# Attention and two MoE layers on one core: products with the weights' high halves first, all low halves on GpSimd, the last logits on TensorE

## The chip, the cores and the metric

The kernel runs on one core of one Trainium2 chip. The metric is the time of one execution on the device in microseconds. Engines go by short names: PE (TensorE, matrix products), DVE (VectorE), ACT (ScalarE), POOL (GpSimd) and SP (SyncE, which issues most DMAs).

## What is computed

Attention over pooled keys and values, then two mixture-of-experts layers (MoE 1 and MoE 2), in float32. 4608 tokens of 512 numbers each go to one of 8 experts; an expert is two matrices, 512 x 1024 and 1024 x 512.

```python
scores = scale * np.matmul(q, k_p.transpose(0, 1, 3, 2))      # k_p, v_p: means over 8 positions
...
logits = x @ w_gate                        # MoE 2: + modality_bias[modality_id]
expert_idx = np.argmax(logits, axis=1)
...
gate_w = probs[np.arange(N), expert_idx]   # probs: softmax of the logits
for e in range(E):
    mask = expert_idx == e
    xe = x[mask]
    h = np.maximum(xe @ w1[e], 0.0)
    ye = h @ w2[e]
    out[mask] = gate_w[mask, None] * ye
```

## The kernel before

**Three products for one.** A float32 matrix is held as a high half (ACT casts it to a shorter form, fp32r) and a low half (the rest, a subtraction on DVE or POOL). x w becomes xh wh + xl wh + xh wl. So each weight block that arrives by DMA in a staging tile is split: `w1h` and `w2h` by ACT (L213, L230), `w1l` and `w2l` by a subtraction (L214, L237). Each has four parts of 128 x 1024. In the tables `W1P` and `W2P` stand the parts made on POOL (0, 1, 2 of `w1l`; 0, 1, 3 of `w2l`); the others are made on DVE.

**Blocks.** The tokens of a MoE lie sorted by expert in DRAM (`XS`). `moe_body` works through blocks of 256 rows; 22 in MoE 1 (numbers 0 to 21) and 19 in MoE 2 for this input. An expert's last block can have 128 rows or fewer (a half block): then only half of the work is done, by another branch. In a block:

- rows of the next block, already in `xq`, are transposed on DVE (`xpose`, L223) to `xt`, and split to `xT` by ACT (L226) and POOL (L227);
- `gemm1`, 96 products of 128 x 256: four `ph` tiles (f2 = 0 to 3) of 24 products each, in three PSUM buffers. After each, ACT makes `hh` (ReLU, high half, L273) and DVE `hl` (low half, L274). Within a `ph` tile the three products of each piece follow each other: w1h xh, w1h xl, w1l xh;
- `gemm1_half`, for a half block: 48 products, and then eight transposes, whose results give `hh` (L256) and `hl` (L259);
- `gemm2(1)` and then `gemm2(0)`, 24 products of 128 x 512 each for rows 128 to 255 and 0 to 127, in the order hh w2h, hh w2l, hl w2h for each of 8 pieces. A half block does only `gemm2(1)`;
- the result, scaled by the gate on ACT (L1067), is scattered by POOL (L153): in MoE 1 to the sorted rows of MoE 2, in MoE 2 to the output.

**Gating of MoE 2** runs inside MoE 1, a block late: 16 logits a block on DVE (`logits2`, L1128, a multiplication by a column of the gate's weights with an accumulator, which reads the `py` result from PSUM), then some eleven small operations on DVE (`gate_a1`, `gate_a2`, `gate_b2`: L110 to L150), with rank products on PE (L135, L138). The tiles between them, and the logits `lgz`, lie in SBUF. In each block the order on DVE is fixed by the order of the code: `LH` = 4 of the 8 logits of one half in one place, the others in a later one. The last block's rows stay in SBUF (`tail`); their logits are made in the first block of MoE 2 by `lg_last`: for rows 0 to 127 by four transposes and four products on PE, for rows 128 to 255 by 8 operations on DVE with both inputs in SBUF.

**Change of weights.** When the next block belongs to another expert, a flag from a table lets the engines take branches that split the new weights: `next_w1`, `next_w2` and, after half blocks (flags `phchg` and `hchg`), some in other places. In MoE 1 this happens ahead of blocks 4, 5, 7, 8, 12, 15, 16 and ahead of MoE 2. Blocks 4, 5, 8, 15 and 16 are half blocks.

**The table.** Which rows and which expert a block has is worked out by some 60 small operations on DVE (`table`, L777 to L880). They stand in block 0 and block 1 of each MoE. `load_chg` and `load_regs` read its results (`nbt`) into registers.

The engines run their own instruction streams in order; where one needs another's result it waits at that instruction, with all that stands behind it.

Of the kernel before, what the change touches and what calls it, by code (L numbers as in the profile page):

```python
# [20 lines left out]
def attn_moe_moe(ctx: ExitStack, tc: tile.TileContext, q, k, v, wg1, w1a, w2a, ids, wg2, bias2, w1b, w2b, out):  # L21
# [86 lines left out]
    def gate_a1(lg, ns, valid, oh=None, go=now, dd=None):  # L108
# [33 lines left out]
    def gate_b2(oh, rk, ns, m, ib, rows, go=now):  # L142
        pa = sp.tile([P, ns, E], F32, name=f"pa{ns}", tag=f"pa{ns}")
# [95 lines left out]
    def gemm1_half(xs, early):  # L239
        for g in range(2):  # L240
            ph = mh.tile([P, 2, BK], F32, name="ph", tag="ph")
            for j in range(2):
# [516 lines left out]
    def table(m):  # L759
# [536 lines left out]
```

## Time and profile before

| | |
|---|---|
| device time, three runs | 1207.57, 1210.95, 1212.03 us (median 1210.95) |
| span of the profiled execution | 1206.5 us |
| PE busy (matmul) | 1101.0 us, 91% |
| DVE busy | 730.3 us, 61% |
| POOL busy | 494.6 us, 41% |
| ACT busy | 375.9 us, 31% |

The profiled execution has one time only, its span. Attention fills the first part of it, MoE 1 runs from there to 760 us, MoE 2 from 765 us to the end. The busy shares are means over all of it; the stretches behind them differ. A group of waits tells how long an engine stood still, at which instruction, and which engine's instruction released it. In a timeline, a number with "x" behind an instruction tells how many stand in the row, and the length is that of the row.

### The profile page before, as it was taken

To read this page: it belongs to the slowest core of one execution; us is meant where nothing else is said; L and a number is where in the kernel's file an instruction comes from. 1 tells how busy PE (TensorE), PEld (TensorE's weight loads), DVE (VectorE), ACT (ScalarE), POOL (GpSimd) and SP (SyncE) were. 2 spreads that over 40 slices of the span, in tenths; PEclk is the share of its full clock that TensorE was granted. 3 is DMA by queue.
4 is the path that set the end of the run, shared out by engine and by line. 5 is a ranking of instruction groups with operands and counts; after the bars stand their busy time and mean duration, and the time that the engine had idled before them with its cause. 6 is when DMAs were issued, how large, how long until landed. Compare 5 with 4: busy or idle time off the path is not lost. (4 is left out here: it accounts for less than half of the span.)

```text
span 1206.5 us, 24663 instructions
## 1 busy us (share of the span) xinstructions
PE 1101.0 (91%) x6985; PEld 971.5 (81%) x6985; DVE 730.3 (61%) x1914; ACT 375.9 (31%) x716; POOL 494.6 (41%) x488
## 2 busy tenths in 40 slices
PE   6979998889986989989978999599999999999997
PEld 5767877768975868978857898588989989989986
DVE  4866776788889887887798868772221223221221
ACT  2433444424253441242351223212212232212211
POOL 5455666654176663162484224512121144121221
PEclk8988999888988989999998999989999999999999
DMA  8999667426357474142171721037212112121121
GB/s 206 251 263 269 179 188 197 169 69 138 93 139 214 111 173 124 50 124 89 43 203 39 184 56 55 22 89 178 54 49 60 37 37 71 37 58 51 37 56 37
DMA packets 148620, 135.63 MB, mean 112 GB/s; under 512 B 62502, under 2 KB 116774, under 8 KB 148272
## 3 DMA queue, kind: packets, MB, share of 16 engines
q1 hardware_dynamic: 138448, 104.68, 35.4%
q0 software_dynamic: 9424, 28.47, 6.7%
q8 instruction: 80, 1.31, 0.5%
q14 instruction: 140, 1.15, 0.3%
q10 hardware_dynamic: 528, 0.02, 0.0%
HBM read 249.30 MB, written 39.31 MB: 239 GB/s over the span
## 5 line engine op out<-in xcount | busy, mean ns | idle before, releaser
L270 PE MATMUL ph<-xT,w1h 128*128 128x256 f32 x2112 | 381.8, 283 | 12.9 <-DVE hl L274 7.0
L270 PEld LDWEIGHTS ph<-xT,w1h 128*128 128x128 f32 x2112 | 329.0, 190 | 18.1 <-DVE hl L274 7.4
L270 PE MATMUL ph<-xT,w1l 128*128 128x256 f32 x1056 | 297.4, 282 | 0.0
L1053 PE MATMUL py<-w2h,hl 128*128 128x512 f32 x608 | 247.0, 406 | 22.4 <-DVE hl L259 20.3
L274 DVE SCALAR_TENSOR_TENSOR hl<-ph,hh 128x512 fp32r<-128x512 f32 x140 | 95.3, 686 | 278.8 <-ACT hh L273 238.8
L1053 PE MATMUL py<-w2l,hh 128*128 128x512 f32 x608 | 244.1, 402 | 5.8 <-POOLq L911 4.6
L1053 PE MATMUL py<-w2h,hh 128*128 128x512 f32 x608 | 245.6, 404 | 0.5 <-ACT hh L256 0.5
L227 POOL TENSOR_TENSOR xT<-xt,xT 128x512 fp32r<-128x512 f32 x78 | 100.2, 1305 | 258.3 <-ACT xT L226 247.8
L270 PEld LDWEIGHTS ph<-xT,w1l 128*128 128x128 f32 x1056 | 200.5, 190 | 0.0
L1128 DVE SCALAR_TENSOR_TENSOR xr<-py,mt,wgt 128x512 f32<-128x512 f32 x284 | 194.4, 745 | 6.6 <-DVEq L911 6.0
L273 ACT ACTIVATE hh<-ph 128x512 fp32r<-128x512 f32 x140 | 83.8, 600 | 291.5 <-PE ph L270 266.7
L1053 PEld LDWEIGHTS py<-w2h,hl 128*128 128x128 f32 x608 | 116.8, 192 | 52.5 <-DVE hl L259 22.4
L153 POOL DMA_INDIRECT XS<-xr,pos x84 | 83.1, 989 | 160.1 <-DVE pos L150 66.3
L1053 PEld LDWEIGHTS py<-w2l,hh 128*128 128x128 f32 x608 | 117.1, 193 | 34.9 <-POOLq L911 5.5
L1053 PEld LDWEIGHTS py<-w2h,hh 128*128 128x128 f32 x608 | 117.1, 193 | 26.0 <-ACT hh L256 0.8
L214 POOL TENSOR_TENSOR w1l<-stage,w1h 128x1024 fp32r<-128x1024 f32 x31 | 74.0, 2404 | 58.8 <-ACT w1h L213 58.1
L1069 POOL DMA_INDIRECT out_dram<-yo,oi x37 | 37.2, 1006 | 136.4 <-POOLq L911 67.4
L321 POOL TENSOR_TENSOR stage<-stage 128x512 f32<-128x512 f32 (+4 forms) x60 | 72.2, 1213 | 24.8 <-DMA stage<-in_v_dram 14.4
L223 DVE STREAM_TRANSPOSE xt<-xq 128x1024 f32<-128x1024 f32 x42 | 52.3, 1244 | 46.9 <-POOLq L911 28.4
L237 POOL TENSOR_TENSOR w2l<-stage,w2h 128x1024 fp32r<-128x1024 f32 x32 | 75.5, 2391 | 6.4 <-ACT w2h L230 6.2
L1067 ACT ACTIVATE yo<-py,mt 128x512 f32<-128x512 f32 x37 | 25.5, 689 | 152.6 <-PE py L1053 147.3
L1067 ACT ACTIVATE xr<-py,mt 128x512 f32<-128x512 f32 x39 | 26.8, 688 | 130.5 <-PE py L1053 125.5
(267 smaller groups left out, 1409.8 us busy)
## 6 DMA issues: line engine op xcount, KB each, us to landing
stage<-in_moe_w_dram SPq DMA_DIRECT2D x196, 512.0 KB
stage<-in_moe_w_dram SPq DMA_DIRECT2D x44, 2048.0 KB
xq<-XS SPq DMA_DIRECT2D x180, 128.0 KB
XS<-zero SPq DMA_DIRECT2D x16, 516.0 KB
qp<-in_q_dram SPq DMA_DIRECT2D x32, 256.0 KB
stage<-in_k_dram SPq DMA_DIRECT2D x7, 1024.0 KB
stage<-in_v_dram SPq DMA_DIRECT2D x7, 1024.0 KB
wgt<-WT SPq DMA_DIRECT2D x1, 2048.0 KB
```

Of the source, the lines that this page charges most:

```text
L153: i = nc.gpsimd.indirect_dma_start(out=XS[m][:], out_offset=bass.IndirectOffsetOnAxis(ap=pos[0 : src.shape[0], s : s + 1], axis=0), in_=sr ...
L214: (eng or nc.vector).tensor_tensor(out=w1l[:, j], in0=wst1[:, :, f], in1=w1h[:, j].bitcast(F32), op=ALU.subtract)
L223: nc.vector.transpose(out=dst[:].rearrange("p c (g i) -> p g c i", i=QP), in_=src[:].rearrange("p g (c j) -> p g c j", c=NC1))
L227: (eng or nc.gpsimd).tensor_tensor(out=dst[:, 1, cs], in0=src[:, cs], in1=dst[:, 0, cs].bitcast(F32), op=ALU.subtract)
L237: (eng or nc.vector).tensor_tensor(out=w2l[c], in0=wst2[:, 2 * c : 2 * c + 2, :], in1=w2h[c][:].bitcast(F32), op=ALU.subtract)
L270: nc.tensor.matmul(ph[:, fc % 2, :], lhsT=lw[:, fc // 2, c, fs], rhs=rx, start=n == 0, stop=n == len(mms) - 1)
L273: nc.scalar.activation(out=hh[f2], in_=ph, func=AF.Relu)
L274: nc.vector.scalar_tensor_tensor(out=hl[f2], in0=ph, scalar=0.0, in1=hh[f2][:].bitcast(F32), op0=ALU.max, op1=ALU.subtract)
L321: (eng or nc.gpsimd).tensor_tensor(out=r[0:pp, sl, 0:w], in0=r[0:pp, sl, 0:w], in1=r[0:pp, sl, w : 2 * w], op=ALU.add)
L1053: nc.tensor.matmul(py, lhsT=lw[fc // 2][:, fc % 2, s * P : (s + 1) * P], rhs=rw[fc // 2][:, fc % 2, :], start=n == 0, stop=n == 3 * NC2 - 1)
L1067: nc.scalar.activation(out=x2[:, s, 0:DM], in_=py, func=AF.Copy, scale=t_[:, s, 0:1])
L1128: V.scalar_tensor_tensor(out=junk[e % 2], in0=py, scalar=sc, in1=wgt[:, e, :], op0=ALU.mult, op1=ALU.mult, accum_out=lgz[:, s, e : e + 1])
```

## The change

1. `gemm1_late` takes the place of `gemm1` in all blocks but the first of MoE 1: all products with `w1h` of f2 = 0, 1, 2 (48), then those with `w1l` of these (24), then high and low of f2 = 3. `gemm1_half` and `gemm2` are written likewise: in `gemm2` 16 products with `w2h`, then 8 with `w2l`.
2. All low halves are made on POOL. `next_w1` makes the four w1 parts in one place, after the block's gemm1 and the split of the next rows; `next_w2` the four w2 parts in one place, after `gemm2(0)`. The places for half blocks, their flags and four operations of the table are gone.
3. The gate's scratch (`lgz`, `lg2`, a copy of `rev`, `m2`, `pa`, `pf`) lies in a PSUM tile `gsc`, so that the operations of the gate have an operand in PSUM.
4. `lg_last` makes the logits of both halves of the last rows on PE.
5. `LH` is 5; the other logits follow after the low products of f2 = 2, or after gemm1 in a half block. In block 0 of MoE 2 gate steps and w2 splits stand at other places.

```diff
+    def gemm1_late(xs, each):
+        phs = {}
+        for low, f2 in ((0, 0), (0, 1), (0, 2), (1, 0), (1, 1), (1, 2), (0, 3), (1, 3)):
+            if not low:
+                phs[f2] = mh.tile([P, 2, BK], F32, name="ph", tag="ph")
+            ph = phs[f2]
+            for h in range(2):
...
+            if low:
+                nc.scalar.activation(out=hh[f2], in_=ph, func=AF.Relu)
+                nc.vector.scalar_tensor_tensor(out=hl[f2], in0=ph, scalar=0.0, in1=hh[f2][:].bitcast(F32), op0=ALU.max, op1=ALU.subtract)
+                each(NC2 + f2)
...
-        def next_w1(*js):
-            if nxt < NB or m == 0:
-                gated(nxt_chg(), lambda: [split_w1(j, nc.gpsimd if j in W1P else None) for j in js])
+        def next_w1():
+            if i > 0 and (nxt < NB or m == 0):
+                gated(nxt_chg(), lambda: [split_w1(j, nc.gpsimd) for j in range(4)])
...
-        if i > 2:
-            gated(phchg, lambda: [split_w2l(c, nc.gpsimd if c in W2P else None) for c in range(4)])
...
+            seq = [(lw, w2h, fc) for fc in range(NC2) for lw in (hh, hl)] + [(hh, w2l, fc) for fc in range(NC2)]
...
-            logits2(1, x[:, 1, 0:DM], 1.0, range(E))
+            for h in range(2):
+                for c in range(NC1):
+                    nc.tensor.transpose(tp[h][:, c * P : (c + 1) * P], x[:, h, c * P : (c + 1) * P], ident)
...
+            for c in range(NC1):
+                nc.tensor.matmul(ps[:, h * E : (h + 1) * E], lhsT=xl[h][:, c * P : (c + 1) * P], rhs=wgb[:, c, :], start=c == 0, stop=c == NC1 - 1)
```

Lines of the kernel after are numbered otherwise: `hh` and `hl` are made at L280 and L281, `w1l` at L211, `w2l` at L234.

Block 1 of MoE 1 on DVE, before: `hl` of the first `ph` tile stands in the middle of the table (names that begin with `t_`, `tab`, `nbt`, `valt`, `invt` are the table's).

```order
549 L836 SCALAR_TENSOR_TENSOR t_l<-t_aj,t_l 128x25
550 L838 TENSOR_SCALAR t_ra<-t_l 128x25
551 L839 SCALAR_TENSOR_TENSOR tab_3061<-t_u,t_ra 128x25
552 L274 SCALAR_TENSOR_TENSOR hl_2845<-ph,hh_2841 128x512
553 L816 TENSOR_TENSOR t_lt<-t_ge,eidx 128x200
554 L818 TENSOR_REDUCE t_e<-t_lt 128x25
555 L816 TENSOR_TENSOR t_lt<-t_ge,t_en 128x200
```

The same place after:

```order
577 L898 TENSOR_TENSOR t_fm<-t_ch,pw_273 128x25
578 L899 TENSOR_REDUCE t_nl<-t_fm 128x1
579 L900 CAST nbt_3064<-t_nl 128x1
580 L901 TENSOR_TENSOR valt_3058<-t_l,slot 128x50
581 L903 TENSOR_SCALAR invt_3060<-valt_3058 128x50
582 L281 SCALAR_TENSOR_TENSOR hl_2845<-ph,hh_2841 128x512
583 L281 SCALAR_TENSOR_TENSOR hl_2846<-ph,hh_2842 128x512
584 L281 SCALAR_TENSOR_TENSOR hl_2847<-ph,hh_2843 128x512
```

All of the table, with the flags in `nbt`, has come ahead of the first `hl`.

A block with a change of weights on DVE, before: one `w2l`, the transpose of the next rows, then the first `hl`.

```order
707 L237 TENSOR_TENSOR w2l_85<-stage,w2h_81 128x1024
708 L911 UNCONDITIONAL_BRANCH x2
709 L223 STREAM_TRANSPOSE xt<-xq_88 128x8x4x32
710 L991 REGISTER_ALU
711 L991 COMPARE_AND_BRANCH
712 L274 SCALAR_TENSOR_TENSOR hl_2845<-ph,hh_2841 128x512
```

After, the first `hl` follows five logits (`xr`, with accumulator in `gsc`), and no `w2l` stands there:

```order
686 L1144 SCALAR_TENSOR_TENSOR xr_91,gsc<-py_3071,mt_95,wgt 128x512
687 L1144 SCALAR_TENSOR_TENSOR xr_90,gsc<-py_3071,mt_95,wgt 128x512
688 L1121 UNCONDITIONAL_BRANCH
689 L281 SCALAR_TENSOR_TENSOR hl_2845<-ph,hh_2841 128x512
690 L281 SCALAR_TENSOR_TENSOR hl_2846<-ph,hh_2842 128x512
```

On POOL, after, the block's start has all four `w2l`, behind a branch:

```order
262 L934 REGISTER_ALU
263 L934 COMPARE_AND_BRANCH
264 L234 TENSOR_TENSOR w2l_83<-stage,w2h_79 128x1024
265 L234 TENSOR_TENSOR w2l_84<-stage,w2h_80 128x1024
266 L234 TENSOR_TENSOR w2l_85<-stage,w2h_81 128x1024
267 L234 TENSOR_TENSOR w2l_86<-stage,w2h_82 128x1024
```

The one of DVE has joined POOL's three.

Block 0 of MoE 2 on DVE, before: the last rows' logits from SBUF (`xr_91`, two of eight shown), then `hl` and the gate's first steps (`lgz`, `lg`).

```order
2992 L1128 SCALAR_TENSOR_TENSOR xr_90,lgz<-xr_91,wgt 128x512
2993 L1128 SCALAR_TENSOR_TENSOR xr_91,lgz<-xr_91,wgt 128x512
2994 L1134 UNCONDITIONAL_BRANCH
2995 L274 SCALAR_TENSOR_TENSOR hl_2845<-ph,hh_2841 128x512
2996 L1210 COPY lgz<-pr 128x8
2997 L1170 SCALAR_TENSOR_TENSOR lg_15151<-bias_t,mlast,lgz 128x8 x2
```

The same place on PE, after (`xr` are the last rows, in one of two buffers by a branch, `hrow` the transposed rows from ACT):

```order
2161 L1219 MATMUL py_3072<-ident,xr_90 128x128 x4
2162 L1219 MATMUL py_3070<-ident,xr_90 128x128 x4
2163 L1150 UNCONDITIONAL_BRANCH
2164 L1219 MATMUL py_3072<-ident,xr_91 128x128 x4
2165 L1219 MATMUL py_3070<-ident,xr_91 128x128 x4
2166 L1150 UNCONDITIONAL_BRANCH
2167 L275 MATMUL ph<-xF,w1h 128x256 x16
2168 L1229 MATMUL pr<-wgb,hrow 128x8 x8
```

The eight logits have moved from DVE to eight transposes and eight small products on PE.

## Rows read from the trace of the kernel before

**Rows 1.** The page, part 2: PE busy tenths in 40 slices of 30.2 us.

```profile
PE   6979998889986989989978999599999999999997
```

**Rows 2.** Busy time (x count) of PE, PEld, DVE, ACT, POOL by stretch; clock, DMA share, GB/s.

```profile
345.76:366.29 20.53, 14.96 (x85) 12.00 (x83) 19.71 (x50) 10.69 (x17) 16.71 (x11) 0.83 0.96 257
366.29:390.07 23.78, 14.96 (x84) 11.96 (x84) 21.60 (x44) 7.94 (x14) 13.79 (x9) 0.78 0.85 220
412.83:441.52 28.69, 25.36 (x148) 22.80 (x147) 24.67 (x61) 12.90 (x17) 19.29 (x13) 0.88 0.70 171
529.14:557.31 28.17, 24.49 (x149) 21.86 (x148) 24.85 (x69) 6.81 (x11) 13.04 (x10) 0.94 0.76 210
557.31:580.00 22.69, 22.69 (x149) 20.31 (x147) 16.86 (x54) 4.92 (x9) 4.75 (x5) 1.00 0.17 44
271.07:300.37 29.30, 27.03 (x145) 23.80 (x146) 24.23 (x71) 12.41 (x31) 15.00 (x12) 0.85 0.59 125
764.84:803.34 38.50, 28.32 (x162) 25.83 (x163) 29.42 (x82) 8.71 (x13) 14.55 (x10) 0.82 0.16 50
```

**Rows 3.** Waits of PE, 300 to 800 us: total, times, longest (us).

```profile
PE py L1053 <- DVE hl L259: 20.3, 5, 6.6
...
PE pr L135 <- DVE oh L122: 10.0, 1, 10.0
...
PE ph L270 <- DVE hl L274: 7.0, 2, 3.7
```

**Rows 4.** Groups by line: tiles, count, busy us, mean ns, idle ahead and releaser.

```profile
L214 POOL TENSOR_TENSOR w1l<-stage,w1h 128x1024 fp32r<-128x1024 f32 x31 | 74.0, 2404 | 58.8 <-ACT w1h L213 58.1 <-POOLq L911 0.5 <-issue 0.2
...
L237 POOL TENSOR_TENSOR w2l<-stage,w2h 128x1024 fp32r<-128x1024 f32 x32 | 75.5, 2391 | 6.4 <-ACT w2h L230 6.2
...
L237 DVE TENSOR_TENSOR w2l<-stage,w2h 128x1024 fp32r<-128x1024 f32 x8 | 38.2, 4778 | 8.7 <-ACT w2h L230 7.0 <-DVEq L1092 0.9 <-ACT hrow L248 0.9
...
L214 DVE TENSOR_TENSOR w1l<-stage,w1h 128x1024 fp32r<-128x1024 f32 x9 | 18.5, 2057 | 4.7 <-issue 2.3 <-ACT xr L1067 1.1 <-ACT w1h L213 0.8
...
L1128 DVE SCALAR_TENSOR_TENSOR xr<-py,mt,wgt 128x512 f32<-128x512 f32 x284 | 194.4, 745 | 6.6 <-DVEq L911 6.0 <-issue 0.4
...
L144 DVE TENSOR_TENSOR pa<-pr,run 128x16 f32<-128x16 f32 x22 | 3.7, 168 | 11.6 <-PE pr L138 7.4 <-DVEq L911 3.7 <-PEq L1092 0.5
...
L146 DVE TENSOR_TENSOR pa<-pa,oh 128x16 f32<-128x16 f32 x22 | 10.0, 453 | 0.0
```

**Rows 5.** Timeline of POOL and DVE in block 7: start, length, count, idle ahead.

```profile
414.33 7.14 POOL L237 TENSOR_TENSOR w2l<-stage,w2h 128x1024 fp32r<-128x1024 f32 x3
...
418.90 3.67 DVE L237 TENSOR_TENSOR w2l<-stage,w2h 128x1024 fp32r<-128x1024 f32 x1
...
424.09 0.65 DVE L274 SCALAR_TENSOR_TENSOR hl<-ph,hh 128x512 fp32r<-128x512 f32 x1
```

**Rows 6.** Timeline of PE, POOL and DVE at the switch to MoE 2.

```profile
764.84 0.55 PE L270 MATMUL ph<-xF,w1h 128*128 128x256 f32 x1 [5.12 <-DVEq L1232]
...
769.69 1.10 POOL L153 DMA_INDIRECT XS<-xr,pos  x1 [10.85 <-ACT hrow L1205]
...
771.75 10.23 DVE L1128 SCALAR_TENSOR_TENSOR xr<-xr,wgt 128x512 f32<-128x512 f32 x1
...
772.08 9.34 POOL L237 TENSOR_TENSOR w2l<-stage,w2h 128x1024 fp32r<-128x1024 f32 x4
```

**Rows 7.** Timeline of ScalarE in block 13, an ordinary full block.

```profile
563.21 0.60 ACT L273 ACTIVATE hh<-ph 128x512 fp32r<-128x512 f32 x1 [2.23 <-PE ph L270]
```

**Rows 8.** Timeline of DVE in block 1 of MoE 1, then of MoE 2.

```profile
277.65 0.69 DVE L274 SCALAR_TENSOR_TENSOR hl<-ph,hh 128x512 fp32r<-128x512 f32 x1 [0.67 <-ACT hh L273]
...
287.75 0.15 DVE L874 CAST nbt<-t_nl 128x1 int32<-128x1 f32 x1
...
813.51 0.15 DVE L874 CAST nbt<-t_nl 128x1 int32<-128x1 f32 x1
```

**Rows 9.** The stretch after PE's gap in block 7; columns as in rows 2.

```profile
423.40:430.20 6.80, 5.41 (x25) 5.41 (x26) 5.22 (x12) 2.00 (x2) 4.67 (x2) 0.50 1.10 318
```

More of the change, by code (lines that the diff above doesn't have):

```diff
@@ L140, in gate_b1, with gate_b2 @@
         return rk
-    def gate_b2(oh, rk, ns, m, ib, rows, go=now):
-        pa = sp.tile([P, ns, E], F32, name=f"pa{ns}", tag=f"pa{ns}")
+    def gate_b2(oh, rk, ns, m, ib, rows, go=now, sc=None):
+        pa = sc[2] if sc else sp.tile([P, ns, E], F32, name=f"pa{ns}", tag=f"pa{ns}")
         go(lambda: nc.vector.tensor_tensor(out=pa, in0=rk[:, 0:ns, :], in1=run[m][:].unsqueeze(1).broadcast_to([P, ns, E]), op=ALU.add))
@@ L259, in gemm1_half @@
                 nc.vector.tensor_tensor(out=hl[f2][:, :, P : 2 * P], in0=pt[:, j], in1=hh[f2][:, :, P : 2 * P].bitcast(F32), op=ALU.subtract)
+    def gemm1_late(xs, each):
[5 more added lines that the diff above has]
+            for h in range(2):
+                fs = slice(h * P, (h + 1) * P)
+                for c in range(NC1):
+                    for z in range(1 if low else 2):
+                        nc.tensor.matmul(ph[:, h, :], lhsT=(w1l if low else w1h)[:, f2, c, fs], rhs=xs[:, z, c, :],
+                                         start=not low and h + c + z == 0, stop=bool(low) and h + c == NC1, skip_group_check=True)
+                if not low:
+                    each(2 * f2 + h)
+            if low:
+                nc.scalar.activation(out=hh[f2], in_=ph, func=AF.Relu)
+                nc.vector.scalar_tensor_tensor(out=hl[f2], in0=ph, scalar=0.0, in1=hh[f2][:].bitcast(F32), op0=ALU.max, op1=ALU.subtract)
+                each(NC2 + f2)
     def gemm1(xs, each):
@@ L967, in each @@
                             second_list() if j == 5 else gate_prev(j)
-                if m == 1 and i == 0 and fc in (0, 2):
-                    for c in (fc, fc + 1):
-                        split_w2(c, nc.gpsimd)
                 if fc == 5 and i == 1:
                     regs[m] = load_chg(m)
-                if fc == 5 and not half and (m == 1 or i != NBMIN - 1):
-                    next_w1(0, 1)
             if half:
@@ L978, in run1 @@
             else:
-                for _ in gemm1(xF if i == 0 else xT, each):
-                    pass
-        if i > 2:
-            gated(phchg, lambda: [split_w2l(c, nc.gpsimd if c in W2P else None) for c in range(4)])
+                gemm1_late(xF if i == 0 else xT, each)
         if i > 1:
@@ L998, in moe_body @@
             xnext()
-        prev = late[0:1]
+        if m == 0 and i == 1:
+            for f in late:
+                f()
         if m == 0 and i > 1:
-            gated((regs[0][4] & (1 << (i - 1))) == 0, prev[0])
-        for f in late[i != 1 :]:
-            f()
+            todo = late[:]
+            gated((regs[0][4] & (1 << (i - 1))) == 0, lambda: [f() for f in todo])
         late.clear()
@@ L1007, in moe_body @@
             wload_b(0, i)
-            next_w1(0, 1)
         if m == 0 and pend:
             pend.pop()()
-        if hchg is not None and (m == 1 or i != NBMIN - 1) or (i == NB - 1 and m == 0):
-            gated(hchg, lambda: [split_w1(j, nc.gpsimd if j in W1P else None) for j in (0, 1)])
+        next_w1()
         if i > 0:
@@ L1091, in moe_body @@
         else:
-            with tc.If(full) as arm:
+            with tc.If(full):
                 second()
-            with arm.Else():
-                if nxt < NB:
-                    live = regs[m][0] > nxt if i >= NBMIN - 1 else None
-                    gated(nxt_chg(), lambda: gated(live, lambda: [split_w2h(c) for c in range(4)]))
+        next_w2()
         if m == 0:
@@ L1166, in f @@
             if j == 0:
-                lg = sp.tile([P, 2, E], F32, name="lg2", tag="lg2")
+                lg = lg2t
                 for o in range(2):
```

130 lines of the change are left out of this document (68 added, 62 removed).

## The prediction

> **What bounds the kernel now.** I read the busy shares by slice first, then busy time by stretch, then the waits of TensorE (PE), then the lines behind them. PE's share stands at nine tenths or more in most slices, and in all but the last of MoE 2 after its start [rows 1], so the change can gain only where PE idles or runs at the lower clock. By stretch that is uneven: a full block of MoE 1 with nothing in its way takes 22.69 us with PE busy for all of it and a granted clock of 1.00, while blocks beside a change of weights take 28.69 and 28.17 us, two half blocks 20.53 and 23.78 us, and the first block of MoE 2 38.50 us [rows 2]. Between 300 and 800 us PE waits longest for hl from VectorE (DVE): 20.3 us in half blocks, 7.0 us in full ones; once it waits 10.0 us for the gate's oh [rows 3].
>
> Behind these waits stands one thing. When the weights change, DVE makes some of the low halves, and it makes them slowly: 4778 ns for w2l, where GpSimd (POOL) needs 2391 [rows 4]. In block 7 the row shows why: DVE's w2l starts at 418.90 and lasts 3.67 us while POOL works on its own three from 414.33 for 7.14; hl, queued behind it, comes at 424.09 [rows 5]. In the first block of MoE 2 a logit of DVE with both inputs in SBUF takes 10.23 us while POOL makes w2l for 9.34 [rows 6]; the logits read from PSUM take 745 ns on average [rows 4]. So DVE with two SBUF inputs stands still while POOL works. After each gap PE also runs at 0.50 of its clock for some microseconds, as at 423.4 to 430.2 [rows 9].
>
> [...]
>
> **The change part by part.** Sums are made against the profiled execution, 1206.5 us; the median of the runs, 1210.95, lies 4.45 above it, and I add that at the end.
>
> *Splits from DVE to POOL.* DVE loses 8 w2l by 4778 ns and 9 w1l by 2057 ns, 56.7 us [rows 4]. POOL gains 17 by 2.40, 40.8 us. Per change POOL then has 4 x 2.40 + 4 x 2.39 = 19.2 us, and with two xT (2.6 us) and two scatters of about 1.1 [rows 4, 6] some 24 us. A full block of 22.69 us, with an ordinary block after it, can swallow that; a half block cannot: its PE work lies between 11.4 us (half a full block) and the 14.96 for which PE is busy in one, half clock included [rows 2]; I take 12.9.
>
> *High halves first.* Per matmul PE takes (2.23 + 0.60)/24 = 0.118 us [rows 7]. In a full block w1l is now needed 48 matmuls, 5.6 us, after the start instead of at once, and w2l 16 matmuls into gemm2. That hides POOL's later finish in lone changes. The price: hh[0] comes after 56 matmuls, 6.6 us, instead of 2.8; and the high pass of the fourth ph tile waits for the first of three buffers, so for hl[0], 72 matmuls or 8.5 us in. hl[0] then comes at about 6.6 + 0.6 + 0.7 = 8.0 us: half a microsecond to spare. DVE has gate operations (1.8 us), five logits (3.4) and a transpose (1.25) ahead of it, 6.4 us, and is in time.
>
> *Blocks 7 and 12*, lone changes in full blocks: 28.69 and 28.17 against 22.69 [rows 2], so 6.0 and 5.5 us to gain. DVE's w2l is gone and hl[0] comes in time. I leave 0.5 each for gate operations that still wait for POOL: **-5.5 and -5.0**.
>
> *Half blocks* (4 and 5; 15 and 16 look alike, and I price them as the first pair): 20.53 + 23.78 = 44.3 us where 2 x 12.9 would do. The wait for hl goes, but POOL's 24 us per change come next, and the DMA share is 0.96 and 0.85 already [rows 2], so weights could hardly come faster than one change in 20 us. Laying POOL's chain out (w2l to 12 us after the start, xT, w1l to 24, scatter, w2l to 36, xT) starts block 6 some 40.6 us in instead of 44.3; a half-clock stretch of its first microseconds takes 2 back. **-1.7 for each pair**, between 0 and -4.3 (DMA's 40 us). Block 8, a lone half, is bound by POOL and DMA: 0.
>
> *The switch to MoE 2.* Now PE stands 5.12 us before 764.84 [rows 6] and 10.0 us for oh [rows 3] in a block of 38.50. The eight logits go to PE (8 transposes and 8 small matmuls, some 1.6 us, and two copies on ScalarE), so oh no longer waits for POOL. PE waits there for DVE's queue, and DVE has no w1l (2057 ns) to make ahead of the exit any more: I let PE start 1.2 us of that earlier, at 763.6. But POOL, with a fourth w1l (2.40) before the exit, of which I let 0.8 vanish in its idle time, comes to its first scatter at about 771.3 instead of 769.69; with 2.3 for each pair of scatters and 2.39 for each w2l it does two w2l to 778.4, the last rows' scatter to 781.2 (0.5 of waiting with it), and two w2l to 786.0. PE is through gemm1 (11.3 us, the 1.6 and 3.4 of lost clock) near 780, needs the last w2l 22 matmuls of gemm2 later, at 785.1, waits 0.9, and ends near 792; xT is ready some 1.5 later. The next block starts at 793.7 instead of 803.34: **-9.6**. If POOL's second pair slips further, each microsecond costs one.
>
> *Gate scratch into PSUM.* It takes gate operations out of POOL's way (L146 averages 453 ns with SBUF operands only; L144, which reads PSUM, 168 [rows 4]). No row shows an accumulator written to PSUM: I take 0, by the logits that already read PSUM; bounds 0 to 0.1 us for each of 16 a block, in 5.8 us of DVE slack (22.69 less 16.86 busy [rows 2]), so 0 on PE. [...]
>
> *Block 1 of each MoE.* The rest of the table, and the load of its flags on ScalarE, now stand ahead of hh[0] and hl[0], which before came at 277.65, in the middle of the table [rows 8]. The flags are written at 287.75; without that hl and its wait, and one table operation, at 286.4; with load, hh and hl, ph is free at 288.7. PE, which starts at 271.07, is through its 72 matmuls at 282.4 (8.5 us and some 2.8 lost to the half clock; the granted clock of the block is 0.85 [rows 2]): 6.3 us idle and a further half-clock stretch, against 29.30 less 27.03, 2.3 us, that it stands there now. Its end moves from 300.4 to about 305: **+4.6** (bounds 2 and 6). In MoE 2 the flags come at 813.51 [rows 8] less the same 1.4, so hl[0] near 814.2 against 811.8 for PE: 2.4 and some lost clock, **+3.5** (1.2 to 5).
>
> *The rest*: removed branches and four table operations, 0.6 us of DVE off the path, 0. In the rest of MoE 2 PE is hardly idle [rows 1], and the order within a product costs nothing: 0.
>
> Sum: -5.5 - 5.0 - 1.7 - 1.7 - 9.6 + 4.6 + 3.5 = -15.4, so 1191.1 profiled, and with 4.45 **1195.6, say 1196 us**.
>
> **The rivals.**
> A, larger gain: the table in block 1 does not hold PE (the loads slip past), and POOL keeps up in the half blocks. Then +8.1 falls away and each pair gains the 4.3 that DMA leaves: 1195.6 - 8.1 - 5.2 = 1182. For it: w1l is needed late. Against it: 24 us of POOL work per half block, and the instruction order of block 1.
> B, a new wait eats the gain: PE waits for POOL where it waited for DVE, since four low halves now come one after the other. Each of the four half blocks costs 2.4 (one more w2l) instead of the -3.4 in all, and the switch keeps 4.8 of its 9.6: 1195.6 + 13.0 + 4.8 = 1213; with one of the two, 1200 to 1209. This is also how the change would fail to do what it says.
> C, slower: the half microsecond between hl[0] and the fourth ph tile is not there. Seventeen full blocks of MoE 1 would each wait; it decides from (15.4 + 6)/17 = 1.3 us a block beyond the margin. A delay of 2 us gives 1195.6 + 34 = 1230. For it: hh[0] comes 3.8 us later than now. Against it: DVE's 5.8 us of slack a block.
>
> **How the numbers follow.** The forecast has 0.56, A 0.14, B 0.22, C 0.08. About 0.5% (6 us) is what a measurement of this kernel can tell from no change. The forecast and A are faster by more than that, and a little of B: 0.72; most of B is within it: 0.19; C and B's end beyond 1217: 0.09. The range goes from A's 1182 to 1213, B's full price.
>
> **What would show it.** Right: DVE has no w1l or w2l; in blocks 7 and 12 PE has no gap over 1 us; block 0 of MoE 2 has no wait for oh and takes about 30 us; block 1 of MoE 1 shows PE waiting some 6 us for hl; the half-block pairs stay above 40 us, with PE waiting for POOL's w1l or w2l. Wrong: ordinary full blocks longer than 22.7 us (C), pairs at 46 us or more (B), or block 1 without its gap (A).

## The result and the profile after

The change makes the kernel slower: median 1225.3 us (four runs, 1221.12 to 1229.5) against 1209.41 (four, 1207.57 to 1212.03), ratio 1.0126 with an interval of 1.0087 to 1.0165. 1196 was predicted, in a range of 1182 to 1213. The profiled execution has a span of 1227.4 us, 20.9 more than before.

Its page, busy time by engine and PE's slices, against [rows 1]:

```profile
PE 1117.5 (91%) x6997; PEld 982.0 (80%) x6997; DVE 738.9 (60%) x1874; ACT 372.9 (30%) x717; POOL 528.3 (43%) x505
...
PE   6989999896997997999978999689999999999997
```

DVE has not become less busy (730.3 us before), although 56.7 us of low halves have left it. The stretches that answer to [rows 2], columns as there: half blocks 4 and 5, block 7, block 12, an ordinary full block (10), block 1 of MoE 1, half block 8, the first block of MoE 2, and an ordinary one of MoE 2.

```profile
365.05:381.17 16.12, 13.06 (x84) 10.56 (x82) 13.05 (x31) 9.11 (x16) 15.65 (x10) 1.00 0.85 198
381.17:405.27 24.10, 17.66 (x84) 14.33 (x84) 22.86 (x40) 11.18 (x18) 22.63 (x14) 0.79 0.83 219
430.50:453.77 23.27, 22.55 (x149) 19.98 (x147) 22.32 (x31) 12.50 (x17) 22.79 (x13) 1.00 0.84 210
546.69:569.95 23.26, 22.56 (x149) 19.98 (x148) 21.62 (x54) 8.71 (x13) 18.36 (x13) 1.00 0.89 242
500.15:523.43 23.28, 22.58 (x149) 20.01 (x147) 20.07 (x56) 4.92 (x9) 4.71 (x5) 1.00 0.13 30
280.66:315.26 34.60, 27.17 (x144) 24.49 (x145) 26.57 (x69) 12.33 (x31) 14.40 (x12) 0.82 0.58 135
453.77:477.24 23.47, 15.41 (x85) 12.61 (x83) 22.18 (x63) 8.61 (x15) 16.89 (x12) 0.78 0.83 212
784.55:825.49 40.94, 30.59 (x175) 27.43 (x175) 19.08 (x65) 8.81 (x14) 15.79 (x16) 0.83 0.15 48
909.46:931.66 22.20, 22.20 (x145) 20.01 (x144) 5.19 (x6) 4.80 (x8) 4.50 (x4) 1.00 0.17 49
```

Blocks 7 and 12 went from 28.7 and 28.2 to 23.3 us, as forecast. But an ordinary full block, 22.69 before, now takes 23.28 with PE busy for 22.58 only. PE's waits from 260 us on (total, times, longest), against [rows 3]:

```profile
PE ph L275 <- DVE hl L281: 26.8, 17, 7.3
PE py L1074 <- DVE hl L263: 7.9, 4, 7.3
PE pr L1229 <- ACT hrow L1224: 7.2, 1, 7.2
PE ph L275 <- ACT xT L223: 5.7, 2, 3.5
PE py L1074 <- POOL w2l L234: 5.1, 5, 1.4
```

PE still waits for `hl`, now mostly in full blocks. Summed over the blocks of the two profiles, from the first product of MoE 1 to the end:

| blocks | before to after, us | forecast |
|---|---|---|
| attention, same code | +9.6 | 0 |
| 7 and 12 | -10.4 | -10.5 |
| pairs 4, 5 and 15, 16 | -8.0 | -3.4 |
| 8 | +4.0 | 0 |
| 21 and first of MoE 2 | 0.0 | -9.6 |
| block 1 of MoE 1, of MoE 2 | +5.3, +3.4 | +4.6, +3.5 |
| twelve other full blocks of MoE 1 (2, 3, 6, 9 to 11, 13, 14, 17 to 20) | +21.6 | 0 |
| rest of MoE 2 | -4.6 | 0 |

Without attention that is +11.4 us. Attention, whose code is the same, takes 233.4 to 244.1 us in the profiles of this case, and no part of the change is in it: a variant of the kernel before (below, with its last logits on PE) has 243.63 us there, also at a clock of 0.88. The kernel before (its clock is the third last number, 0.93):

```profile
0.00:234.39 234.39, 199.58 (x1351) 169.60 (x1351) 163.17 (x479) 96.30 (x255) 137.83 (x203) 0.93 0.82 211
```

The kernel after, with 0.88:

```profile
0.00:243.96 243.96, 213.61 (x1351) 181.57 (x1352) 168.21 (x479) 95.87 (x255) 138.07 (x203) 0.88 0.81 203
```

So 9.6 of the 20.9 us between these two executions say nothing of the change; below, block lengths are compared, not spans. (The medians lie 15.9 us apart; only the profiled executions can be split by block.)

### The profile page after: what moved, and what is told of

It is laid out like the page before. It is cut to its first block, busy times and chain, and to the rows that moved or that the text cites. A ratio compares the mean times of both kernels' runs of the same rounds, so it can differ in the third digit from the quotient of the medians.

```text
span 1227.4 us, 23353 instructions
## 1 busy us (share of the span) xinstructions
PE 1117.5 (91%) x6997; PEld 982.0 (80%) x6997; DVE 738.9 (60%) x1874; ACT 372.9 (30%) x717; POOL 528.3 (43%) x505
## 5 line engine op out<-in xcount | busy, mean ns | idle before, releaser
L275 PE MATMUL ph<-xT,w1h 128*128 128x256 f32 x2112 | 266.9, 285 | 35.7 <-DVE hl L281 26.8
L275 PEld LDWEIGHTS ph<-xT,w1h 128*128 128x128 f32 x2112 | 258.5, 194 | 44.9 <-DVE hl L281 30.1
L281 DVE SCALAR_TENSOR_TENSOR hl<-ph,hh 128x512 fp32r<-128x512 f32 x136 | 91.1, 690 | 265.2 <-ACT hh L280 262.8
L1144 DVE SCALAR_TENSOR_TENSOR xr<-py,mt,wgt 128x512 f32<-128x512 f32 x284 | 212.3, 748 | 9.5
L280 ACT ACTIVATE hh<-ph 128x512 fp32r<-128x512 f32 x136 | 81.1, 600 | 306.1 <-PE ph L275 268.3
L1074 PE MATMUL py<-w2l,hh 128*128 128x512 f32 x608 | 158.3, 398 | 5.2 <-POOL w2l L234 5.1
L1074 PEld LDWEIGHTS py<-w2l,hh 128*128 128x128 f32 x608 | 112.5, 188 | 33.6 <-POOL w2l L234 7.8
L275 PE MATMUL ph<-xT,w1l 128*128 128x256 f32 x1056 | 132.5, 278 | 0.0
L275 PEld LDWEIGHTS ph<-xT,w1l 128*128 128x128 f32 x1056 | 126.7, 190 | 0.0
L234 POOL TENSOR_TENSOR w2l<-stage,w2h 128x1024 fp32r<-128x1024 f32 x40 | 94.4, 2396 | 8.6 <-ACT w2h L227 8.5
L211 POOL TENSOR_TENSOR w1l<-stage,w1h 128x1024 fp32r<-128x1024 f32 x40 | 94.6, 2396 | 0.2 <-ACT w1h L210 0.2
L1088 ACT ACTIVATE yo<-py,mt 128x512 f32<-128x512 f32 x37 | 25.5, 689 | 156.1 <-PE py L1074 151.6
L1088 ACT ACTIVATE xr<-py,mt 128x512 f32<-128x512 f32 x39 | 26.8, 688 | 138.2 <-PE py L1074 129.2
```

The costliest lines, as they stand in the source:

```text
L211: (eng or nc.vector).tensor_tensor(out=w1l[:, j], in0=wst1[:, :, f], in1=w1h[:, j].bitcast(F32), op=ALU.subtract)
L234: (eng or nc.vector).tensor_tensor(out=w2l[c], in0=wst2[:, 2 * c : 2 * c + 2, :], in1=w2h[c][:].bitcast(F32), op=ALU.subtract)
L275: nc.tensor.matmul(ph[:, h, :], lhsT=(w1l if low else w1h)[:, f2, c, fs], rhs=xs[:, z, c, :], start=not low and h + c + z == 0, stop=bool( ...
L280: nc.scalar.activation(out=hh[f2], in_=ph, func=AF.Relu)
L281: nc.vector.scalar_tensor_tensor(out=hl[f2], in0=ph, scalar=0.0, in1=hh[f2][:].bitcast(F32), op0=ALU.max, op1=ALU.subtract)
L1074: nc.tensor.matmul(py, lhsT=lw[fc // 2][:, fc % 2, s * P : (s + 1) * P], rhs=rw[fc // 2][:, fc % 2, :], start=n == 0, stop=n == len(seq) - 1)
```

## The experiments

### The accumulator in PSUM

A logit is two instructions on DVE: the multiplication, and DVE_READ_ACCUMULATOR, which writes the sum to `lgz`. In block 10 after the change, DVE (start, length, operation; in brackets the idle time ahead of a row and what ended it) and the wait of PE:

```profile
505.19 0.75 DVE L1144 SCALAR_TENSOR_TENSOR xr<-py,mt,wgt 128x512 f32<-128x512 f32 x1
505.86 0.14 DVE L1144 DVE_READ_ACCUMULATOR xr<-py,mt,wgt 128x1 f32 x1
506.04 0.75 DVE L1144 SCALAR_TENSOR_TENSOR xr<-py,mt,wgt 128x512 f32<-128x512 f32 x1
...
508.42 0.14 DVE L1144 DVE_READ_ACCUMULATOR xr<-py,mt,wgt 128x1 f32 x1
508.42 1.91 DVE L281 SCALAR_TENSOR_TENSOR hl<-ph,hh 128x512 fp32r<-128x512 f32 x3
...
509.19 1.54 PE L275 MATMUL ph<-xT,w1h 128*128 128x256 f32 x11 [0.70 <-DVE hl L281]
```

The logits start 0.85 us apart (505.19, 506.04). In the same block of the kernel before, such pairs start 0.67 apart:

```profile
483.88 0.74 DVE L1128 SCALAR_TENSOR_TENSOR xr<-py,mt,wgt 128x512 f32<-128x512 f32 x1
...
484.55 0.74 DVE L1128 SCALAR_TENSOR_TENSOR xr<-py,mt,wgt 128x512 f32<-128x512 f32 x1
```

After the change, DVE gets to `hl[0]` 8.27 us after the block's start (500.15), and three `hl` in a row show that `hh` has long been waiting. The first run puts only the accumulators back into SBUF.

```diff
-    lgz = gsc[:, 0 : 2 * E].rearrange("p (s e) -> p s e", e=E)
+    lgz = mp.tile([P, 2, E], F32, name="lgz")
```

> The kernel after, with one thing put back: the logits' accumulators lie in SBUF again; the rest of the gate's scratch stays in PSUM. Theory A (the accumulator in PSUM is what makes DVE late): logits stand 0.68 us apart instead of 0.85, the nine logits and the transpose ahead of the first hl end 1.6 us earlier, PE's 0.7 us wait for hl in each ordinary full block of MoE 1 is gone (block 22.3 us instead of 23.3), and blocks 2, 6, 17 and 18 lose most of their 2.5 to 5 us; in all some 15 us less than the kernel after, about 1210. Theory B (hl is late because hh comes late, high halves first): the 0.7 us stay and the time stays within 3 us of the kernel after.

Measured: 1199.81 us, ratio to the kernel before 0.9909 (0.9884 to 0.9934). Block 10, then DVE's last accumulator and `hl[0]` in it:

```profile
480.16:502.56 22.40, 22.40 (x149) 20.03 (x148) 18.33 (x56) 4.92 (x9) 4.71 (x5) 1.00 0.14 32
```

```profile
486.32 0.09 DVE L1144 DVE_READ_ACCUMULATOR xr<-py,mt,wgt 128x1 f32 x1
487.50 1.51 DVE L281 SCALAR_TENSOR_TENSOR hl<-ph,hh 128x512 fp32r<-128x512 f32 x2 [1.09 <-ACT hh L280]
```

Now DVE is free 6.24 us into the block, waits 1.09 for `hh` and starts `hl[0]` at 7.34; PE has no gap. One operand's place turns the change from 1.3% slower into 0.9% faster (some 15 us less than the kernel after were expected, 25.5 came). By block it gives back 18.3 of the 21.6 us of the twelve full blocks, and 8.0 in block 8 (23.47 to 15.48), of which more below. Blocks 6, 9 and 17, each behind a half block, stay long: 24.11, 24.40 and 25.47 us against 22.8 before; what holds them was not tested. The converse, on the kernel before: its last logits all on PE for both halves (first run), and that with the accumulators in PSUM (second, which alone has the last two lines).

```diff
...
-            logits2(1, x[:, 1, 0:DM], 1.0, range(E))
+                for h in range(2):
+                    nc.tensor.transpose(tp[h][:, c * P : (c + 1) * P], x[:, h, c * P : (c + 1) * P], ident)
...
+    gsc = mq.tile([P, 512], F32, name="gsc")
+    lgz = gsc[:, 0 : 2 * E].rearrange("p (s e) -> p s e", e=E)
```

> The kernel before with the logits of both halves of the last rows on PE, as in the kernel after. Theory A (DVE's logits waiting out POOL hold the gate's oh): PE's 10.0 us wait goes, block 0 of MoE 2 falls from 38.5 to some 29 us, about 1202. Theory B (POOL's w2l bind next): 33 us or more.

> The kernel before with the last rows' logits on PE (as in before_pelogits, 1211) and the logits' accumulators in PSUM; splits and the order of products as before. Theory A (the price is DVE time, 0.18 us a logit and 2.8 us a block, and it costs only where DVE's queue is what PE waits for): logits 0.85 us apart, but with each hl due only 8.5 us after the first hh's products PE waits little for it in ordinary blocks, so they stay within 0.2 us of 22.7; beside changes of weights 1 to 3 us more; about 1215 to 1222. Theory B (it costs wherever it stands): 0.6 us in each ordinary block of MoE 1, as in the kernel after, about 1230.

Measured: 1211.25 us, 0.9973 (0.995 to 0.9997), and 1217.6, 1.0062 (1.004 to 1.0083): 0.9% for the accumulators (the second run also gives the transposes of `lg_last` another PSUM tile; that block keeps its length, 34.97 and 34.84 us). PE's logits alone take the first block of MoE 2 from 38.50 to 34.97 us only, where some 29 were expected. With the accumulators in PSUM an ordinary block (490.08) keeps its 22.69 us although DVE works 1.8 us more in it; most of the cost, 0.9 to 2.1 us each, comes in blocks 5, 7, 12, 15 and 18 to 20 (block 19 is the second row). In 7, 12 and 18 to 20 PE's added wait is for DVE; in 5 and 15 it is for POOL, and why it grows there was not followed:

```profile
490.08:512.77 22.69, 22.69 (x148) 20.32 (x147) 19.73 (x57) 4.92 (x9) 4.73 (x5) 1.00 0.15 35
702.88:726.43 23.55, 22.97 (x148) 20.29 (x147) 19.56 (x56) 5.02 (x9) 5.23 (x9) 1.00 0.27 70
```

So the price is the accumulator's. That it hits every block after the change is put down to the new order, which made `hl[0]` of each block a deadline, and to DVE's queue, where five logits of a row now stand ahead of `hl[0]`; before, four stood behind it. No run separates these two.

### The table in block 1

The rest of the table goes behind the first `hl`, the load of its flags behind the third `hh`.

```diff
-                if i == 1 and fc == 1:
+                if i == 1 and fc == NC2:
...
-                if fc == 5 and i == 1:
+                if fc == 7 and i == 1:
```

> The kernel after, with the rest of the table of block 1 (each MoE) behind the first hl, and the load of its flags behind the third hh. Theory A (the table ahead of hl holds PE): PE's 7.3 us wait in block 1 of MoE 1 falls to 2 us or less and the 1.4 us one in MoE 2 goes; with the half clock behind them blocks 1 are about 29 and 22.5 us, some 8 us less in all, about 1217. Theory B (PE would wait for the flags anyway, or ScalarE's plog work holds hh): under 2 us.

Measured: 1218.93 us, 1.0063 (1.0043 to 1.0083). Block 1 of MoE 1 and of MoE 2, and PE's wait in the second:

```profile
270.12:301.09 30.97, 26.65 (x144) 23.50 (x145) 28.49 (x71) 12.46 (x31) 14.41 (x12) 0.86 0.54 110
807.98:836.52 28.54, 25.69 (x145) 22.47 (x145) 14.05 (x47) 5.28 (x9) 4.50 (x4) 0.88 0.63 140
```

```profile
824.84 0.50 PE L1074 MATMUL py<-w2h,hl 128*128 128x512 f32 x1 [2.57 <-DVE hl L281]
```

34.60 becomes 30.97 (29 expected), so the table is what held PE in MoE 1. In MoE 2 the remedy fails: 25.89 becomes 28.54 (22.5 expected), since `hl[1]` to `hl[3]` now stand behind the table and gemm2 waits for them.

### The copies behind the casts at the switch

As the trace has it, POOL's fourth `w1l` ends the chain of the old MoE; SP, whose next loads go into the same staging tile, issues its eight DMAs only then; the exit follows; ACT's first cast waits, and the copies of the transposed rows stand behind it. The run below tests the last link alone; the first ones are read from who released whom. POOL, SP, ACT and PE after the change, with what each waited for:

```profile
775.69 9.44 POOL L211 TENSOR_TENSOR w1l<-stage,w1h 128x1024 fp32r<-128x1024 f32 x4
...
785.16 4.08 SPq L193 DMA_DIRECT2D stage<-in_moe_w_dram  x8
...
793.28 1.99 ACT L227 CAST w2h<-stage 128x1024 fp32r<-128x1024 f32 x2 [9.46 <-SPq L1250]
795.18 1.06 ACT L1224 COPY hrow<-py 128x512 f32<-128x512 f32 x2
...
795.81 3.58 PE L1229 MATMUL pr<-wgb,hrow 128*128 128x8 f32 x16 [7.16 <-ACT hrow L1224]
```

The run puts the first two splits of `w2` behind the call that issues these copies.

```diff
                         gate_prev(2)
-                        split_w2(0, nc.gpsimd)
-                        split_w2(1, nc.gpsimd)
                     if fc in (0, 2):
                         next(late[0], None)
+                    if fc == 0:
+                        split_w2(0, nc.gpsimd)
+                        split_w2(1, nc.gpsimd)
```

> The kernel after, with ScalarE's two copies of the last rows ahead of its two casts of w2 in block 0 of MoE 2. Theory A (the copies queue behind casts that wait for SP's exit, SP for POOL's fourth w1l): PE's 7.2 us wait for the copies goes, PE runs its gemm1 meanwhile, block 0 falls from 41 to some 33 us unless POOL's w2l, which still start after 794, come next; 4 to 8 us less, about 1219. Theory B (everything waits for the exit of SP, whatever stands first): no gain, 1225.

Measured: 1215.67 us, 1.0026 (1.0003 to 1.0048). The block falls from 40.94 to 33.33 us; the copies are in time, and PE next waits for `hl`, which stands behind an operation of the gate, L127 (789.18 to 793.13; next experiment):

```profile
778.40:811.73 33.33, 28.31 (x174) 25.48 (x174) 20.50 (x65) 8.70 (x14) 15.78 (x16) 0.90 0.19 58
```

```profile
793.97 3.78 PE L275 MATMUL ph<-xF,w1h 128*128 128x256 f32 x16 [3.83 <-DVE hl L281]
```

### One gate operation left in SBUF

L127 of the gate, a tensor_scalar, kept input and output in SBUF (`se`). Ahead of half block 8 it meets a run of POOL with no gap, two halves of `xT` and four of `w1l`:

```profile
444.62 12.01 DVE L127 TENSOR_SCALAR se<-se 128x2 f32<-128x2 f32 x1
...
444.61 2.54 POOL L224 TENSOR_TENSOR xT<-xt,xT 128x512 fp32r<-128x512 f32 x2
447.11 9.49 POOL L211 TENSOR_TENSOR w1l<-stage,w1h 128x1024 fp32r<-128x1024 f32 x4
...
468.29 0.79 PE L1074 MATMUL py<-w2h,hl 128*128 128x512 f32 x1 [7.29 <-DVE hl L263]
```

It ends at 456.63, with the last of the run (456.60), and PE waits for the `hl` behind it. That L127 keeps both operands in SBUF is not enough for this, though. In the run with the accumulators in SBUF `se` lies in SBUF as well, and L127 of block 7 meets the same run of POOL. But DVE comes to it 0.73 us into the run's first operation, not at its start as after the change (444.62 and 444.61), and gets in at the end of that operation:

```profile
430.40 2.56 POOL L224 TENSOR_TENSOR xT<-xt,xT 128x512 fp32r<-128x512 f32 x2
...
431.13 0.59 DVE L127 TENSOR_SCALAR se<-se 128x2 f32<-128x2 f32 x1
```

Block 8 then takes 15.48 us. So the loss there needs both, operands in SBUF and the moment at which DVE comes to them. The run moves `se` into the PSUM tile.

```diff
...
-        gate_a2(dpend, 2, gate)
+        gate_a2(dpend, 2, gate, se=gsc[:, 100:102])
```

> The kernel after, with the gate's sum (the operand of the addition before the reciprocal) in PSUM too. Theory A (this one operation, SBUF to SBUF with a single operand, waits out POOL's whole row of low halves): its 10.6 and 12.0 us in blocks 4 and 7 become 0.2, the half block after block 7 falls from 23.5 to about 17.5 us (its 7.3 us wait for hl goes), blocks 4 and 5 gain 1 to 3; 6 to 10 us in all, about 1217. Theory B (POOL and DMA bound the half blocks): that operation becomes short but the half blocks keep their lengths within 1 us.

Measured: 1224.12 us, 1.0114 (1.0066 to 1.0162). L127 takes 0.17 us at this place, and half block 8 falls from 23.47 to 16.13:

```profile
448.36:464.49 16.13, 13.49 (x84) 10.74 (x83) 12.66 (x32) 8.56 (x15) 15.65 (x11) 1.00 0.79 169
```

The time hardly moved all the same (some 1217 us expected), since the blocks of MoE 2 grew from 22.2 to 22.6 or 22.7 us, 8.3 in all: the tile removed had shifted `xT` by 64 bytes (below).

### All low halves on POOL, in the kernel before

```diff
-    W1P = (0, 1, 2)
-    W2P = (0, 1, 3)
+    W1P = (0, 1, 2, 3)
+    W2P = (0, 1, 2, 3)
```

> The kernel before with all low halves on POOL, each at its old place. Theory A (DVE's splits behind POOL's are what makes hl late): blocks 7 and 12 lose 5 us each, the two pairs of half blocks 2 to 4 each, some 12 to 16 us in all, about 1197. Theory B (with each low half needed at once, PE waits for POOL's fourth instead): the waits for hl go, waits for w1l and w2l come, within 4 us of the kernel before.

Measured: 1200.08 us, 0.9889 (0.9858 to 0.9921). These two table entries alone take block 12 from 28.17 to 23.62, 5 and 16 from 23.8 to 17.8 and 18.4, and 7 from 28.70 to 25.55; block 8 grows from 19.46 to 21.96. Over all blocks that is -12.5 us. Blocks 7 and 12:

```profile
410.93:436.48 25.55, 23.59 (x148) 20.21 (x147) 21.49 (x63) 12.59 (x17) 22.13 (x14) 1.00 0.80 191
526.59:550.21 23.62, 23.23 (x149) 20.37 (x148) 22.25 (x73) 6.81 (x11) 16.50 (x12) 1.00 0.99 257
```

### The address of xT

In MoE 2 PE is busy without a gap before and after, with as many products, and still a block takes 22.51 or 22.20 us. The products of gemm1 start 117.7 ns apart before and 114.3 after. What differs for them is where `xT` lies: 384 bytes above a multiple of 512 in each partition's SBUF before, at a multiple of 512 after (the weights `w1h`, `w1l` at 64 above one in both). The first run adds a 128-byte tile ahead of `xT` to the kernel before; three more move `xT` or the weights in the best version (next section).

```diff
+    mp.tile([P, 32], F32, name="pad")
     xT = mp.tile([P, 2, NC1, BK], F32R, name="xT")
```

> The kernel before with 128 unused bytes a partition ahead of xT, so that xT (the moving operand of gemm1) starts at a multiple of 512 bytes in each partition, as it happens to do in the kernel after (171520; before 171904, in the run with the sum in PSUM 171456). Theory A (the place of xT sets the pace of gemm1's products: 114.3 ns apart at a multiple of 512, 117.7 at 384 above one, 119.8 at 448 above): products 114.3 ns apart, a full block of MoE 2 takes 22.2 instead of 22.5 us, the whole some 12 us less, about 1199. Theory B (the new order of the products is what made them faster): no change, 1211.

Measured: 1202.08 us, 0.9896 (0.987 to 0.9921), for 128 bytes that nobody reads.

This changes what the runs above mean. The change put `xT` where this run has it, so this is the kernel to hold it against: the change is then some 2.3% slower (1.0126 against 0.9896), and with the accumulators in SBUF no faster (0.9909 against 0.9896). Its gain of 0.9% over the kernel before is about what the address gives. Nor does a run show a gain from the high halves first: the run before this one, all low halves on POOL, reaches 0.9889 with the old order and the old address.

The next is the best version (next section) with the weights and `xF` at multiples of 512 as well:

```diff
+    ct([P, 112], F32, "padw")
     w1h = ct([P, 4, NC1, 2 * P], F32R, "w1h")
...
+    ct([P, 8], F32, "padx")
     xF = ct([P, 2, NC1, BK], F32R, "xF")
...
```

> As best1 (1177), with the weight tiles and xF moved too, so that w1h, w1l, w2h, w2l and xF start at multiples of 512 bytes in each partition, like xT (best1 has the weights at 64 above one). Theory A (the place of every moving operand counts): gemm2's products of 512 columns, 233 ns apart now, come down to 229 or less, 0.2 us a block and 8 us in all, about 1169. Theory B (64 above a multiple is as good, or it counts for the 256-column operand only): no change, 1177.

Measured: 1187.75 us, 0.9817 (0.979 to 0.9844), slower than without it (0.9688): 120.0 ns. Neither 1169 nor 1177 us came. So the start of `xT` alone does not decide. Two more test the distance of `xT` from the weights (only the size of the tile ahead of `xT` differs):

> best2 with xT 64 bytes lower: the weights w1h, w1l still start at a multiple of 512 bytes of the partition, xT starts at 448 above one, so that xT lies as far from the weights, modulo 512, as in the kernel after and best1 (weights at 64, xT at 0). Theory A (what counts is the distance of the moving operand from the weights): two 256-column products of gemm1 114 ns apart as in best1, ordinary full blocks of MoE 1 22.3 us, some 1177 us. Rival B (what counts is the start of xT itself, and best2 was slow for some other of its moved tiles): 119 to 120 ns apart, blocks 22.9 us, some 1187 us, as in best2.

> best1 with xT 64 bytes higher: weights at 64 above a multiple of 512 bytes, xT also at 64, so that their distance modulo 512 is 0 as in best2. Theory A (the distance counts): 120 ns apart as in best2, ordinary full blocks 22.9 us, some 1187 us. Rival B (only the start of xT counts, and only a multiple of 512 bytes is fast): also slower than 114 ns, but with no reason for 120.0 in particular; 117 to 118 ns as for the kernel before would do as well.

Measured in one run each: 1184.04 and 1194.02 us (attention 237.2 and 244.1 of them). An ordinary block of MoE 2, length and PE's busy time first, in five kernels.

The kernel before:

```profile
861.68:884.19 22.51, 22.51 (x145) 20.32 (x144) 5.19 (x6) 4.81 (x8) 4.51 (x4) 1.00 0.17 49
```

With 128 bytes more:

```profile
860.07:882.18 22.11, 22.11 (x145) 19.92 (x144) 5.19 (x6) 4.79 (x8) 4.49 (x4) 1.00 0.17 50
```

The weights at multiples of 512:

```profile
835.03:857.73 22.70, 22.70 (x145) 20.51 (x144) 5.18 (x6) 4.79 (x8) 4.49 (x4) 1.00 0.17 49
```

`xT` 64 bytes lower than that:

```profile
837.58:860.09 22.51, 22.51 (x146) 20.30 (x144) 5.18 (x6) 4.80 (x8) 4.50 (x4) 1.00 0.17 49
```

The best version with `xT` 64 bytes higher:

```profile
844.27:866.97 22.70, 22.70 (x146) 20.51 (x144) 5.18 (x6) 4.79 (x8) 4.50 (x4) 1.00 0.18 49
```

PE is busy throughout at a clock of 1.00 in all five; the pace differs.

| xT mod 512 | weights mod 512 | ns from product to product | kernels |
|---|---|---|---|
| 0 | 64 | 114 | after, before with 128 bytes more, best |
| 384 | 64 | 117.7 | before |
| 448 | 64 | 119.8 | `se` in PSUM |
| 64 | 64 | 119.9 | last run |
| 0 | 0 | 120.0 | weights moved |
| 448 | 0 | 117.5 | weights and xT moved |

The distance theory held for distance 0 (120 in both) and fell for 448 (114 in one, 117.5 in the other). Neither operand's start nor their distance settles the pace alone; what the rule is stays open.

### What the remedies give together

The change with the accumulators in SBUF, the copies first, `se` in PSUM with 64 bytes ahead of `xT` to hold its address, and the old order of gemm1 in the two blocks 1:

> The kernel after with four things mended: accumulators in SBUF, ScalarE's copies of the last rows ahead of its casts of w2, the gate's sum in PSUM (xT kept at a multiple of 512 bytes by 64 unused bytes), and block 1 of each MoE with the old order of products (so that the first hl comes early again). If the four act one by one: acc_sbuf's 1200, less 7 in block 0 of MoE 2, less 5 and 3 in the blocks 1, less 1 to 2 in the half blocks: about 1183. If DVE's queue or POOL's bind next in the same places: 1190 to 1198.

Measured: 1176.96 us (1176.48 to 1178.94), 0.9688 (0.9661 to 0.9715), 3.1% below the kernel before, and some 2.1% below the kernel before with 128 bytes more. Blocks 1 and 8 of MoE 1 and the first of MoE 2:

```profile
274.49:302.51 28.02, 25.31 (x144) 22.43 (x145) 24.93 (x69) 12.27 (x31) 15.12 (x12) 0.90 0.57 118
434.79:450.18 15.39, 13.07 (x84) 10.59 (x83) 13.90 (x43) 8.50 (x15) 14.90 (x10) 1.00 0.83 170
744.45:774.31 29.86, 26.58 (x174) 23.07 (x174) 20.32 (x65) 8.59 (x14) 15.76 (x16) 1.00 0.20 65
```

## Why the prediction was wrong

The forecast was -15.4 us; the blocks gave +11.4. Of the 26.8 us between them 21.6 lie in the twelve full blocks, 9.6 at the switch and 4.0 in block 8; the pairs and the rest of MoE 2, 4.6 us better than forecast each, took some of it back.

**The step that failed first: the accumulator's price and its cover.** The prediction took 0 for an accumulator written to PSUM, bounds 0 to 0.1 us, and covered it with 5.8 us of idle time on DVE a block. Its price is 0.18 us for each logit behind another (0.85 against 0.67 us apart). The cover was wrong in kind: idle time of the whole block was set against work that stands ahead of `hl[0]`, where half a microsecond was left by the prediction's own count. The numbers of that count were good for accumulators in SBUF, DVE free at 6.4 (measured 6.24) and `hl[0]` done at 8.0 (8.03), but partly by luck: not gate operations stand first in the block, but the end of a row of eight logits from the block before. With the five after the transpose that is thirteen logits, eleven of them behind another, so DVE comes to `hl[0]` 2.0 us later (8.27 against 6.24); it had 1.09 us to spare, and in an ordinary block PE then waits 0.70. The twelve blocks came out 21.6 us longer, 0.1 to 5.3 each, of which the accumulators' return to SBUF took 18.3 back.

Rival C named the place and the missing margin, with a later `hh[0]` as the sign for it; the cause was DVE's queue. That 1225 is near C's 1230 is luck: C took a longer block of 2 us in each of seventeen (sixteen, as block 0 keeps the old order), where ordinary ones came out 0.6 longer and a few 4 to 5.

In block 17 the gap cost more than its length: the wait is 3.16 us, the block 5.3 us longer. PE's granted clock is 0.58 from 669.20, where the wait ends, to 672.60, and 1.00 after that.

**The switch.** -9.6 was forecast, 0.0 came. PE starts earlier, by 2.4 us where 1.2 was forecast (it waits 1.46 us ahead of the block, 5.12 before), but the block takes 40.94 us instead of some 30, which only the best version reaches (29.86). The prediction counted the fourth `w1l` ahead of the exit as 2.4 us, of which 0.8 vanishes, and did not follow who waits for its staging tile: SP, with eight DMAs (4.08 us) and the exit behind them. It put two copies on ACT and did not look at what is queued ahead of them there. The copies alone are 7.6 us (40.94 to 33.33); the 3.8 after them is `hl` behind L127 (3.95 us), a wait that the best version, with `se` in PSUM as well, has down to 0.24.

**Block 8.** 0 was forecast, +4.0 came. The prediction took DVE's trouble for one of two SBUF inputs, and did not look at L127, which has one SBUF input. Moved into PSUM the same operation took 0.17 us and the block 16.13. But with the accumulators in SBUF, and `se` still there too, L127 took 0.59 us and the block 15.48: a shift of 0.7 us in when DVE comes to L127 does as much. The wait itself, 12.01 us over six instructions of POOL for an operation with one SBUF input, was left out of the prediction; that it struck just here was chance.

**Block 1 of each MoE.** Right in mechanism and size: PE waits 7.29 us for `hl` until 299.31 (6.3 forecast), +5.3 and +3.4 against +4.6 and +3.5. In MoE 2 the wait itself is 1.38 us, of 2.4 forecast; the lower clock (0.93 in that block) makes up for it.

**Blocks 7, 12 and the pairs.** Right at 7 and 12 (-10.4 against -10.5), by the cause named: with DVE's halves on POOL and nothing else, 7 gains 3.2 and 12 gains 4.6. Where the other 2.6 come from was not separated. The pairs gained 8.0, near rival A's bound of 8.6. They take 40.2 and 39.5 us, where POOL's chain was laid out to 40.6; it did not hold block 4 (16.12 us), but in block 5 (24.10) PE waits 1.0 and 1.6 us for `w1l`. The 2 us that the forecast took back for lost clock in the block behind a pair are not in this row: blocks 6 and 17, at clocks of 0.93 and 0.94, stand among the twelve. The kernel before with all low halves on POOL, in the old order, gains 10.2 in the pairs, so the new order is not what brought it.

**The order within a product costs nothing** was nearly right: 22.40 against 22.29 us for the same pace of `xT`. That the change shifts `xT` and with it the pace of gemm1, worth 0.3 to 0.4 us in each full block, no row of before could tell; it hid part of the loss, some 12 us by the run with 128 bytes more.

**The gate's scratch in PSUM.** The gate's operations on the PSUM tile take 0.17 to 0.18 us, most of them, and took 0.16 to 0.20 in SBUF where POOL did not hold them; where it did, before, L112 took 2.22 us (756.66 to 758.88, beside POOL's `w1l` from 756.44 to 758.84).

## What to carry to other kernels

Slack counts only up to the deadline: sum the queue ahead of the instruction that someone waits for, not the idle time of the block, and when a new order makes a deadline tighter, price every edit on that queue against it. Of a step moved past a branch or an exit, follow who waits for the buffer that it frees, and what stands in the queue ahead of the instructions it brings. Before a small difference in a dense loop is explained by the edit, look whether the edit has moved an operand's address: a few unused bytes are a cheap test.

## What the runs showed of the hardware

- The accumulator's read takes 141 ns with its target in PSUM and 83 in SBUF (medians of 284). In SBUF the next logit starts with it (both at 479.15 with the accumulators in SBUF), in PSUM 0.18 us after the read's start (505.86 and 506.04, after); an `hl` starts with it in PSUM too (508.42). After, then with the accumulators in SBUF (least, median and most, in ns):

```profile
L1144 DVE DVE_READ_ACCUMULATOR xr<-py,mt,wgt x284: 131/141/144, 307.3 to 772.3; 128x1 f32 x142
```

```profile
L1144 DVE DVE_READ_ACCUMULATOR xr<-py,mt,wgt x284: 73/83/94, 299.6 to 738.5; 128x1 f32 x142
```

- An operation of 2 numbers per partition on DVE, SBUF to SBUF, waited out POOL's run of six instructions, 12.01 us, when it came as the run's first instruction started. In another run it came 0.73 us into that instruction and got in at its end, after 0.59 us. What decides between the two is open.
- In the kernels of the table on `xT` products of 256 columns follow each other 114 to 120 ns apart, 5%, by where their operands lie in SBUF; the granted clock is 1.00 in their ordinary blocks of MoE 2.
